# A conv, two gated expert layers on one core: the sums of the weights' maxima leave their PSUM bank by a ScalarE copy

## The chip, the core and the metric

The kernel runs on one core of a Trainium2 chip. The metric is the device time of one execution, in microseconds (us). A core has five engines that run their own queues of instructions in order: TensorE (PE in the profile, with its weight loads as PEld), VectorE (DVE), ScalarE (ACT), GpSimd (POOL) and SyncE (SP, which issues most of the DMAs). They wait for each other by semaphores. TensorE writes its results into PSUM, which has eight banks per partition; all of them are taken here.

## What is computed

```python
out  = causal_conv(x, softmax(weight))         # 8 heads of 24 columns, 7 taps, x is 4 x 3584 x 192
x    = out.reshape(14336, 192)
# layer 1: every row goes to its best of 8 experts
e    = argmax(x @ w_gate)
x    = softmax(x @ w_gate)[e] * (relu(x @ w1[e]) @ w2[e])          # 192 -> 1024 -> 192
# layer 2: the same, and a sigmoid of a second gate
e    = argmax(x @ w_gate2)
out  = softmax(x @ w_gate2)[e] * sigmoid(x @ w_output_gate)[e] * (relu(x @ w1b[e]) @ w2b[e])
```

## The kernel before

Floats are carried as pairs of float16 (a high and a low part), so that a product is three matmuls of 16 bit. For this the weights of all 16 experts (two layers of eight) are split on the core into two halves each, scaled by a power of two that is found from their largest absolute value. One such half (w1 or w2 of an expert) is a unit of `preps`: it is loaded (L273 to L276), ACT takes absolute maxima along the rows (L298, two pieces, tile `wam`), `scale` finds the power of two, ACT and POOL (in the conv also DVE) write the two halves (L325 to L338), SP stores them.

`scale` calls `total` (L140 to L146): two matmuls with a matrix of ones (L145) add the row maxima of the 128 partitions, so that every partition has the sum. The sum, one number a partition, stands in a PSUM tile `total` with tag `lg` of the pool `rps`. `pow2` then makes the scale on the vector engine: a maximum with a tiny number (L131), which reads the sum, then two bit operations (L136, L137). In the conv there are 16 such units (layer 1), in layer 1's expert slots another 16 (layer 2). `gate_weights` calls `total` twice more (`gaam` at the start, `gbam` in the conv; there the first reader is L133).

The tag `lg` has one buffer, one PSUM bank. In turn it holds:
- `total`, freed by its reader L131;
- in the conv, `lg`: the logits of 4 tiles (matmuls L517), freed by DVE's L532;
- in layer 1's slots, `tp`: six transposes of an earlier slot's result (L1186), freed by ACT's copy `ext` (L1192), and `lg`: that result's logits for layer 2 (L1200), freed by DVE's L1211.

A matmul that writes the bank waits until the tile that it held before has been read.

There are three stages. The **conv** (to about 231 us of the trace) runs 32 turns; in turn k TensorE does the conv of tile group k+1 (L465, tile `cxp`, two buffers), then `total` where a unit is at that point, transposes of group k-3 (L507) and logits of group k-4 (L517). DVE scales group k out of `cxp` (L479 to L487, tile `cxs`); L487 frees the buffer that group k+2 wants. ACT makes `chl` from `cxs` (L493, group k-1) and copies transposes out (L510, `cxt`).

The **slots of layer 1** (63, from about 250 us) and of **layer 2** (63 more) are 256 rows of one expert each, or 128 rows. In slot u TensorE runs stage 1 (L1134, 40 matmuls into four banks `ph`), `total` if a unit is due (every third slot), the transposes `tp` of slot u-3, stage 2 of slot u-1 (L1150, 48 matmuls into `py`, two buffers) and the logits `lg` of slot u-4. ACT and DVE empty each `ph` bank (L1136, then L1137), and ACT and DVE bring the result of slot u-1 to the next layer's form (L1160 to L1168). DVE's routing work, which decides what rows later slots take (L613 to L1021), is woven in between: a little after each stage 1, before the unit's L131. The order of all queues is fixed when the program is written (`manual_schedule`): no engine passes over a waiting instruction.

Of the kernel before, what the change touches and what calls it, by code (L numbers as in the profile page):

```python
# [11 lines left out]
F32 = mybir.dt.float32  # L12
# [5 lines left out]
P = 128  # L18
# [37 lines left out]
class Kern:  # L56
# [83 lines left out]
    def total(self, ams):  # L140

        n = ams[0].shape[-1]
        r = self.rps.tile([P, n], F32, tag="lg", name="total")
        for i, am in enumerate(ams):
            self.nc.tensor.matmul(r, lhsT=self.ones32, rhs=am, start=i == 0, stop=i == len(ams) - 1)  # L145
        return r  # L146

    def setup(self):
        nc = self.nc
# [1298 lines left out]
```

## Time and profile before

| | us |
|---|---|
| three runs: median (lowest to highest) | 1367.17 (1366.86 to 1368.79) |
| the profiled execution | 1367.8 |
| its span, first to last instruction | 1366.1 |
| TensorE busy in the span | 1216.8 (89%) |
| VectorE busy | 827.8 (61%) |
| ScalarE busy | 638.2 (47%) |
| GpSimd busy | 614.4 (45%) |

Busy time is what an engine's instructions took; time in which an engine sits before an instruction is named with the instruction that ended the wait (the releaser). "PE tp L1186 <- DVE wst L131" reads: TensorE stood before the matmul that writes `tp`, and L131's end let it go. An engine that is not the bottleneck may sit idle at no cost, so a wait counts only where its engine is the one that the end hangs on.

### The profile page before, as it was taken

What the parts mean: (1) busy time and instruction counts of PE and PEld (TensorE: products, weight loads), DVE (VectorE), ACT (ScalarE), POOL (GpSimd) and SP (SyncE); (2) the same over time, 40 slices, a digit from 0 to 9 for tenths busy, and PEclk for the clock granted to TensorE, in tenths of its full rate; (3) what the DMA queues carried; (4) which work ended last, traced back from release to release, by engine and by line L of the source; (5) the groups of instructions that cost most, each with busy time, mean ns of one, the idle gap of its engine ahead of it and who ended that gap; (6) DMA issues with size and microseconds to landing.
All of it is one profiled execution on the core that took longest, in us unless ns stands there. A gap on an engine that the chain in (4) does not pass through costs nothing. (4 is left out here: it accounts for less than half of the span.)

```text
span 1366.1 us, 36343 instructions
## 1 busy us (share of the span) xinstructions
PE 1216.8 (89%) x13048; PEld 1151.6 (84%) x13048; DVE 827.8 (61%) x2497; ACT 638.2 (47%) x1155; POOL 614.4 (45%) x673
## 2 busy tenths in 40 slices
PE   5867885788998998998787999999999998999997
PEld 4867885687998898997777999999999997899987
DVE  4677689577777655555477775578665444444433
ACT  2756674254655565654554444433333333333332
POOL 5434442324555454453544434344444446344442
PEclk9556555799999999999998999999999999999999
DMA  6989775455556746695684698664344666655374
GB/s 191 276 218 258 200 213 161 117 127 144 138 138 174 185 111 152 163 256 136 179 212 123 163 223 201 155 139 109 92 118 111 152 148 161 159 138 153 93 195 150
DMA packets 251600, 223.12 MB, mean 163 GB/s; under 512 B 144558, under 2 KB 221031, under 8 KB 251416
## 3 DMA queue, kind: packets, MB, share of 16 engines
q1 hardware_dynamic: 231068, 184.32, 51.2%
q0 software_dynamic: 17136, 34.68, 11.8%
q8 instruction: 107, 1.75, 0.6%
q10 hardware_dynamic: 3212, 1.74, 0.5%
q14 instruction: 77, 0.63, 0.2%
HBM read 275.60 MB, written 60.37 MB: 246 GB/s over the span
## 5 line engine op out<-in xcount | busy, mean ns | idle before, releaser
L1134 PE MATMUL ph<-mxt,wb 128*128 128x256 f16 (+1 forms) x4840 | 536.9, 271 | 21.6 <-DMA mxt<-row 10.1
L1134 PEld LDWEIGHTS <-wb 128*128 128x128 f16 x4840 | 457.4, 99 | 74.9 <-issue 12.1
L1150 PE MATMUL py<-wb,h 128*128 128x192 f16 x5592 | 492.4, 249 | 0.0
L1137 DVE SCALAR_TENSOR_TENSOR h<-ph,h 128x512 f16<-128x512 f32 x476 | 314.2, 687 | 286.7 <-ACT h L1136 281.3
L1150 PEld LDWEIGHTS <-h 128*128 128x128 f16 x5592 | 471.9, 99 | 3.4 <-issue 0.3
L1136 ACT ACTIVATE h<-ph 128x512 f16<-128x512 f32 x476 | 274.3, 595 | 176.4 <-PE ph L1134 171.5
L1050 POOL DMA_INDIRECT row<-rec,idx x238 | 233.1, 979 | 87.6 <-issue 44.1
L1233 POOL DMA_INDIRECT out_dram<-o,io x119 | 121.1, 1017 | 232.4 <-ACT o L1232 193.2
L1169 POOL TENSOR_TENSOR ehl<-exs,ehl 128x256 f16<-128x256 f32 (+1 forms) x63 | 42.1, 667 | 296.9 <-ACT ehl L1168 230.5
L1164 ACT ACTIVATE exs<-py,ess 128x192 f32<-128x192 f32 x119 | 44.0, 418 | 204.6 <-DVE ese L137 195.4
L1232 ACT ACTIVATE o<-py,sc 128x192 f32<-128x192 f32 x119 | 44.0, 417 | 199.7 <-PE py L1150 153.0
L465 PE MATMUL cxp<-x,tz 118*112 118x96 f32 x512 | 90.2, 359 | 43.0 <-DVE cxs L487 34.1
L465 PEld LDWEIGHTS cxp<-x,tz 118*112 118x112 f32 x512 | 83.8, 265 | 45.6 <-DVE cxs L487 36.3
L1160 DVE TENSOR_REDUCE eam<-py 128x2 f32<-128x384 f32 (+1 forms) x63 | 33.6, 533 | 124.0 <-PE py L1150 123.9
L338 POOL TENSOR_TENSOR wh<-wr,wh 128x768 f16<-128x768 f32 x48 | 81.2, 1691 | 54.1 <-ACT wh L326 52.8
L1186 PE MATMUL tp<-ident,ehl 128*128 128x128 f16 x357 | 31.8, 226 | 44.6 <-DVE wst L131 43.3
L510 ACT COPY cxt<-ctp 128x1344 f16<-128x1344 f16 x32 | 40.9, 1277 | 60.8 <-PE ctp L507 60.5
L1192 ACT COPY ext<-tp 128x768 f16<-128x768 f16 (+1 forms) x63 | 47.4, 752 | 45.4 <-PE tp L1186 43.6
L1186 PEld LDWEIGHTS <-ehl 128*128 128x128 f16 x357 | 26.9, 104 | 46.9 <-issue 46.1
L494 POOL TENSOR_TENSOR chl<-cxs,chl 112x512 f16<-112x512 f32 x32 | 37.8, 1183 | 41.7 <-ACT chl L493 37.3
L298 ACT ACTIVATE none<-wr 128x768 f16<-128x768 f32 x64 | 53.7, 839 | 1.0
L517 PE MATMUL lg<-gawt,cxt 128*112 128x16 f16 x384 | 35.0, 226 | 5.8 <-DVE L L532 4.7
(203 smaller groups left out, 1087.1 us busy)
## 6 DMA issues: line engine op xcount, KB each, us to landing
wb<-wd SPq DMA_DIRECT2D x126, 768.0 KB
wb<-wda SPq DMA_DIRECT2D x126, 512.0 KB
wb<-wdb SPq DMA_DIRECT2D x126, 256.0 KB
wb<-wdb SPq DMA_DIRECT2D x126, 128.0 KB
wr<-in_moe_w_dram SPq DMA_DIRECT2D x16, 768.0 KB
wd<-wh SPq DMA_DIRECT2D x16, 768.0 KB
rec<-chl SPq DMA_DIRECT2D x32, 336.0 KB
rec<-ehl SPq DMA_DIRECT2D x56, 192.0 KB
```

The source lines that it names most:

```text
L298: nc.scalar.activation(none, u.r[:, c * CH : (c + 1) * CH], AF.Abs, scale=scale, accum_out=u.am[:, c : c + 1])
L338: nc.gpsimd.tensor_tensor(u.h[:, 1, q], u.r[:, q], u.h[:, 0, q], ALU.subtract)
L465: nc.tensor.matmul(to[:, :, hh * GD : (hh + 1) * GD], lhsT=self.tz[: self.KI, h, :], rhs=xin[b0][: self.KI, o : o + G, h * GD : (h + 1) * GD],
L1050: nc.gpsimd.indirect_dma_start(out=rw[:, :], out_offset=None, in_=rec[:, :], in_offset=bass.IndirectOffsetOnAxis(ap=idx, axis=0))
L1134: nc.tensor.matmul(ph[:, k, :], lhsT=l, rhs=xt[:, xb, 0:n], start=i == 0, stop=i == 4)
L1136: nc.scalar.activation(hi, ph, AF.Relu)
L1137: nc.vector.scalar_tensor_tensor(lo, in0=ph, scalar=0.0, in1=hi, op0=ALU.max, op1=ALU.subtract)
L1150: nc.tensor.matmul(py[:, c, 0:D], lhsT=h[:, f, a, c * P : (c + 1) * P], rhs=w[:, b, f, :], start=n == 0, stop=n == 3 * NCH - 1)
L1164: nc.scalar.activation(xs[:, c], py[:, c], AF.Copy, scale=sc[:, c : c + 1])
L1186: nc.tensor.transpose(tp[:, 3 * c + b], hl[:, c, b * P : (b + 1) * P], self.ident)
L1192: nc.scalar.copy(xt, self.sl[u].pop("tp"))
L1233: nc.gpsimd.indirect_dma_start(out=outs[q % NOUT][:, :], out_offset=bass.IndirectOffsetOnAxis(ap=io[:, 0:1], axis=0), in_=o, in_offset=Non ...
```

## The change

`total` no longer returns the PSUM tile. ACT copies it into a small tile `sums` in SBUF (tags `total1` and `total2` by width, four buffers each), and `total` returns that; so L131 and L133 read `sums`. All lines behind are three higher in the changed kernel (L1186 is L1189, L493 is L496).

```diff
@@ def total(self, ams)
             self.nc.tensor.matmul(r, lhsT=self.ones32, rhs=am, start=i == 0, stop=i == len(ams) - 1)
-        return r
+
+        t = self.ew.tile([P, n], F32, tag=f"total{n}", name="sums")
+        self.nc.scalar.copy(t, r)
+        return t
```

ACT has 34 instructions more, one for each call of `total`; on the other engines the order of the arithmetic, the matmuls and the DMAs is as before, and only what they wait for differs. ACT's queue at the first unit in layer 1's slots, before (`exs` and `ehl` are the result of the slot before last, `h` the four `ph` banks, `ext` the copy that frees the transposes):

```order
L1168 CAST ehl<-exs 128x2x192 [waits Activation_49]
L1136 ACTIVATE h<-ph 128x2x256 [waits PE_49] x4
L1192 COPY ext<-tp_3471 128x768 [waits PE_49]
L1164 ACTIVATE exs<-py,ess 128x192 [waits DVE_49,PE_49,Pool_49]
L1164 ACTIVATE exs<-py,ess 128x192
```

and the same place of the changed kernel:

```order
L1171 CAST ehl<-exs 128x2x192 [waits Activation_49]
L1139 ACTIVATE h<-ph 128x2x256 [waits PE_49] x4
L148 COPY sums<-total 128x1 [waits PE_49]
L1195 COPY ext<-tp_3509 128x768 [waits PE_49]
L1167 ACTIVATE exs<-py,ess 128x192 [waits DVE_49,PE_49,Pool_49]
```

The copy stands behind the slot's four `h` and ahead of `ext`. TensorE's queue there, before:

```order
L1134 MATMUL ph<-mxt,wb_0_70 128x256
L145 MATMUL total<-wam,ones_155 128x1 [waits Activation_49]
L145 MATMUL total<-wam,ones_155 128x1
L1186 LDWEIGHTS ehl
L1186 MATMUL tp_3471<-ident,ehl 128x128 [waits DVE_49]
```

and now:

```order
L1137 MATMUL ph<-mxt,wb_0_70 128x256
L145 MATMUL total<-wam,ones_155 128x1 [waits Activation_49]
L145 MATMUL total<-wam,ones_155 128x1
L1189 LDWEIGHTS ehl
L1189 MATMUL tp_3509<-ident,ehl 128x128 [waits Activation_49]
```

No row moved; the first transpose waits for ACT where it waited for DVE. In the conv, ACT's queue around one of layer 1's units (`chl` of group k-1, `cxt` of group k-3), before:

```order
L493 CAST chl<-cxs 112x4x192 [waits DMAHW3_49,DVE_49]
L510 COPY cxt<-ctp 128x1344 [waits PE_49]
L493 CAST chl<-cxs 112x4x192 [waits DMAHW6_49,DVE_49]
L510 COPY cxt<-ctp 128x1344 [waits PE_49]
L325 ACTIVATE wr<-wr,wss 128x768 [waits DVE_49]
```

and now:

```order
L496 CAST chl<-cxs 112x4x192 [waits DMAHW3_49,DVE_49]
L513 COPY cxt<-ctp 128x1344 [waits PE_49]
L148 COPY sums<-total 128x1 [waits PE_49]
L496 CAST chl<-cxs 112x4x192 [waits DMAHW6_49,DVE_49]
L513 COPY cxt<-ctp 128x1344 [waits PE_49]
```

The copy went ahead of the `chl` of its turn. DVE's queue at that unit has the same rows in the same order in both; its L131, which waited for TensorE, now waits for ACT.

## Rows read from the trace of the kernel before

**Rows 1.** Stages: from:to, length, busy us (count) of PE, PEld, DVE, ACT, POOL, granted clock, DMA share, GB/s.
```profile
277.00:745.00 468.00, 416.38 (x4632) 391.96 (x4630) 304.14 (x922) 252.04 (x481) 225.21 (x233) 0.95 0.63 162
745.00:1366.00 621.00, 602.22 (x6699) 568.23 (x6697) 330.65 (x1085) 239.01 (x467) 273.74 (x290) 0.99 0.60 147
```

**Rows 2.** Waits from 277 to 745 us: waiting <- releaser: total us, times, longest.
```profile
PE tp L1186 <- DVE wst L131: 43.3, 16, 6.9
```

**Rows 3.** Timeline, first unit in the slots: start us, duration us, instruction [idle before <- releaser].
```profile
286.18 0.50 PE L145 MATMUL total<-wam,ones 128*128 128x1 f32 x4
286.22 2.47 DVE L1137 SCALAR_TENSOR_TENSOR h<-ph,h 128x512 f16<-128x512 f32 x4
286.38 0.60 ACT L1136 ACTIVATE h<-ph 128x512 f16<-128x512 f32 x1 [0.49 <-PE ph L1134]
...
290.80 0.15 DVE L131 TENSOR_SCALAR wst<-total 128x1 f32<-128x1 f32 x1
291.00 0.59 PE L1186 MATMUL tp<-ident,ehl 128*128 128x128 f16 x6 [4.32 <-DVE wst L131]
...
296.95 0.30 PE L1200 MATMUL lg<-gbwt,ext 128*128 128x32 f16 x6
```

**Rows 4.** Timeline, third unit in the slots.
```profile
352.75 2.25 ACT L1136 ACTIVATE h<-ph 128x512 f16<-128x512 f32 x4
...
354.65 0.58 PE L145 MATMUL total<-wam,ones 128*128 128x1 f32 x4
...
355.97 0.49 PE L1186 MATMUL tp<-ident,ehl 128*128 128x128 f16 x6 [0.74 <-DVE wst L131]
...
360.26 0.30 PE L1200 MATMUL lg<-gbwt,ext 128*128 128x32 f16 x6
```

**Rows 5.** Timeline, last unit in the slots.
```profile
732.31 2.05 ACT L1136 ACTIVATE h<-ph 128x512 f16<-128x512 f32 x4
...
732.44 0.50 PE L145 MATMUL total<-wam,ones 128*128 128x1 f32 x4
...
739.84 0.80 PE L1186 MATMUL tp<-ident,ehl 128*128 128x128 f16 x6 [6.89 <-DVE wst L131]
...
746.72 0.30 PE L1200 MATMUL lg<-gbwt,ext 128*128 128x32 f16 x6
```

**Rows 6.** Timeline, the fifteenth unit: the longest stall after which stage 2 kept its pace.
```profile
706.25 0.33 PE L1186 MATMUL tp<-ident,ehl 128*128 128x128 f16 x3 [3.36 <-DVE wst L131]
...
706.41 4.12 PE L1150 MATMUL py<-wb,h 128*128 128x192 f16 x48
```

**Rows 7.** Stage view of the six us behind the first stall (columns as in rows 1).
```profile
291.00:297.00 6.00, 6.00 (x56) 5.83 (x56) 0.43 (x4) 0.80 (x1) 0.00 (x0) 0.72 0.01 3
```

**Rows 8.** Groups of ACT by line and form: count | busy us, mean ns | idle before <- releaser.
```profile
L1164 ACT ACTIVATE exs<-py,ess 128x192 f32<-128x192 f32 x119 | 44.0, 418 | 204.6 <-DVE ese L137 195.4 <-PE ph L1134 9.2
L768 ACT ACTIVATE zs<-zs 128x16 f32<-128x16 f32 x7 | 1.4, 200 | 0.0
```

**Rows 9.** Waits from 32 to 231 us, the conv (columns as in rows 2).
```profile
DVE wst L131 <- PE total L145: 29.1, 14, 4.0
```

**Rows 10.** Timeline, one conv turn with a unit.
```profile
43.06 0.83 ACT L493 CAST chl<-cxs 112x768 f16<-112x768 f32 x1 [0.38 <-DVE cxs L487]
...
43.08 3.30 PE L465 MATMUL cxp<-x,tz 118*112 118x96 f32 x16 [1.05 <-DVE cxs L487]
...
46.17 0.91 PE L145 MATMUL total<-wam,ones 128*128 128x1 f32 x4
...
47.11 0.16 DVE L131 TENSOR_SCALAR wst<-total 128x1 f32<-128x1 f32 x1 [3.96 <-PE total L145]
...
50.19 0.69 PE L465 MATMUL cxp<-x,tz 118*112 118x96 f32 x2 [0.93 <-DVE cxs L487]
```

**Rows 11.** Timeline, a conv turn in which ACT is busy when the sum ends.
```profile
109.37 0.53 PE L145 MATMUL total<-wam,ones 128*128 128x1 f32 x4
...
110.23 0.19 ACT L298 ACTIVATION_READ_ACCUMULATOR none<-wr 128x1 f32 x1
```

## Prediction, made before the changed kernel was run

> **What bounds the kernel now.** I read the stages first [rows 1]. Layer 2's slots (745 to 1366 us) have TensorE busy for 602.22 of 621 us at a granted clock of 0.99: whatever arrives there earlier ends earlier. Layer 1's slots with units in them (277 to 745 us) have TensorE busy for only 416.38 of 468 us, at 0.95; DVE is busy for 304.14, so over the whole stretch it is no bound. The list of waits says where most of the missing 51.6 us are: 43.3 us, in 16 waits, TensorE stood before the transposes `tp` until DVE's L131 [rows 2]. There are 16 units there, so every one stalls TensorE once.
>
> The first shows how [rows 3]. The sum ends at 286.68 (start and duration of `total`). The transposes want the same bank, and it is free only when L131 has read the sum. L131 stands in DVE's queue behind four L1137 (2.47 us) and routing work, and starts at 290.80; TensorE goes on at 291.00, 4.32 us late. The reader itself takes 0.15 us: the stall is DVE's queue. It is 0.74 us where DVE had nothing else [rows 4] and 6.89 us where routing was long [rows 5].
>
> A long stall costs more than its own time. Behind the first one the granted clock is 0.72 over six us [rows 7], a mixture of the levels 1.2 and 2.4 GHz. From the transposes to the logits L1200 it takes 5.95 us [rows 3], against 4.29 in the undisturbed slot [rows 4]: 1.66 lost; behind the longest it takes 6.88, 2.59 lost [rows 5]. Five stalls, of 4.32 us and more, are of this kind (I took the same difference for each: 1.66, 1.79, 1.97, 2.68, 2.59; 10.7 in all). Behind a stall of 3.36 us stage 2 took 4.12 us at full pace [rows 6]. [...]
>
> **Part one, layer 1's slots: the bank is freed by ACT.** ACT's queue has the copy behind the slot's four `h`, whose last waits for the same stage 1 as the sum does. So TensorE resumes at the later of two times (the sum's end, plus 0.03; the end of ACT's last `h`), plus the copy, plus the hand to TensorE. That hand is 0.05 us (L131 ends at 290.95, the transposes start at 291.00) [rows 3].
>
> The copy, 128x1 out of PSUM, is not in the trace. Its ends: ACT's 128x16 takes 0.20 us and its accumulator read of one column 0.19; ACT's 128x192 out of PSUM takes 0.418 [rows 8, 11]. One column is nearest to the first, I take 0.20, and keep 0.19 and 0.42 for the range. The Trainium skill prices it otherwise: "ScalarE: Activation LUTs", section "Rules for kernel authors", gives about 0.3 us for an ACTIVATE plus a little per element and tells to use VectorE, not ScalarE, for simple arithmetic; by 0.3 us the final sum would be about 3 us worse than by the row. The 0.20 of the 128x16 speaks against that price, and DVE's cheap 0.15 is just what arrives late here.
>
> With 0.20 the 16 new stalls come in three kinds, from the times of each unit as in [rows 3 to 5]:
> - ACT is free when the sum ends, 3 units: 0.03 + 0.20 + 0.05 = 0.28 us (the row: ACT done at 355.00, sum at 355.23 [rows 4]; one of the three is 0.31). Together 0.87.
> - ACT is at its last `h`, 10 units: in the first, ACT ends at 286.98, so TensorE resumes at 287.23, 0.55 us after the sum [rows 3]; the others 0.54 to 0.74. Together 5.9.
> - ACT is late because the slot before kept it, 3 units: in the last, ACT ends at 734.36, TensorE resumes at 734.61, 1.67 us after the sum [rows 5]; the other two 2.2 and 2.3. Together 6.1.
>
> That leaves 12.9 of 43.3 us: **30.4 saved**. No new stall reaches 3.36 us, so the five slow stretches go too: **10.7 saved**.
>
> Does the gain stay? After the transposes TensorE has stage 2 and the logits, 4.29 us [rows 4], before it writes the first `ph` bank again, which DVE's L1137 must have emptied. In the first unit those four end at 288.69 [rows 3], while TensorE would be there at about 291.6; L131 and what is behind it now delay only DVE's own next step, which waits for stage 2 anyway. TensorE's next demand on that bank comes a whole stage 1 later. So I let it all stand. ACT loses nothing: behind the copy stands `ext`, which waits for the transposes in any case.
>
> **Part two, the conv: one more station on a path that already waits.** Here DVE stands before L131 until TensorE's sum ends, 29.1 us in 14 waits [rows 9], and behind L131 in its queue are the scaling steps whose last, L487, TensorE's next conv group waits for. One turn shows the loop closed [rows 10]: L465 starts at 43.08 when L487 lets it, the sum follows, L131 at 47.11, L465 again at 50.19 when the next L487 lets it. The copy comes between sum and L131: 0.20 + 0.05 for 14 units and for the second gate's sum, 15 x 0.25 = 3.75 us. In one turn ACT still is at its absolute maxima when the sum ends (109.90 against 110.42 [rows 11]), another 0.5. In two units DVE came later than the copy will, and nothing is lost. **4.3 us lost**; 0 if the clock or DVE's idle time covers it, 7.6 with a copy of 0.42. At the start `gaam`'s copy stands behind a DMA issue on ACT's queue, but its result is wanted by the first logits only, more than 10 us later: nothing.
>
> The parked copy also holds back `chl`, which stood ahead of it: from 43.06 to about 47.4 [rows 10]. POOL finishes `chl` some 2.7 us after ACT starts it, so at about 50, and the `cxs` buffer that it frees is wanted by the L487 after next, at about 55: covered.
>
> **Sum.** 30.4 + 10.7 - 4.3 = 36.8 us off the profiled execution's 1367.8 (span 1366.1 and 1.7 around it): 1331.0. The median is 0.6 lower, so 1330.4 against it; I say 1331. With a copy of 0.42 us: 16 x 0.22 = 3.5 less in the slots, 3.3 more in the conv, 1337.8. With no loss in the conv: 1326.7.
>
> **The rivals.**
> - *The stall moves on.* DVE is still behind in the long cases, and TensorE meets it at its next wait for DVE, or, running 9% denser, meets its weights' loads. Then the long five give back what they save (19.0 us of the 30.4: 3.8, 2.8, 4.1, 3.1, 5.2) and keep their slow clock: 36.8 - 19.0 - 10.7 = 7.1 saved, 1361; half of that, 1346. For it: DVE's queue was long for up to 6.9 us. Against: the cover of 4.29 us and a whole stage 1 of 4.5 us before the bank is wanted again; the DMA share of 0.63 [rows 1].
> - *Slower: the copy parks ACT in the conv.* ACT waits at the copy for TensorE while `chl`, POOL and the `cxs` buffers wait behind it. If DVE then waits for a buffer in each of the 16 turns, 2.6 us a turn pay back the whole 41.1; at 3 us a turn: +48 - 41 = +7, 1375. For it: `chl` starts 4.3 us later in that turn [rows 10]. Against: the slack of some 5 us worked out above.
> - *The bank isn't freed sooner.* If ACT came as late as DVE, the stalls stay and only the conv pays: 1372. In 13 of the 16 units ACT was done within 0.5 us of the sum, and the queue has nothing between `h` and copy. As the kernel would then be slower, it counts there.
> - *Only a small gain from the conv's jitter* (within 0.2%, some 2.7 us, which is about what a measurement tells from no change): needs a mixture of the above.
>
> **How the numbers follow.** My forecast 0.78, with its own range of 1325 to 1339; the stall moves on, 0.14 (faster in either half); slower by the parked ACT or an unfreed bank, 0.05; no difference, 0.03. So faster 0.92, same 0.03, slower 0.05. The range of 8 in 10 is 1323 to 1347: 3 us under the forecast without a loss in the conv, since the remaining stalls may come out shorter, and up to half of the moved stall.
>
> **What would show it.** In the trace after: the wait of `tp` names ACT's `sums`, 16 times, 13 us instead of 43.3; the copy's mean is near 0.20 us; the granted clock in layer 1's slots rises from 0.95 to about 0.98; in the conv L131 waits for `sums`, some 33 us; the first L1134 comes 4 us later and layer 2's slots have the length that they had. I am wrong if L131's wait is replaced by one for L1137, L1211 or a load in the slots behind, if L487 waits for POOL or ACT in the conv, or if the copy takes 0.4 us.

## The result, and the profile after

| | before | after |
|---|---|---|
| runs: median (lowest to highest), us | 1367.3 (1366.86 to 1368.79), 4 runs | 1326.91 (1326.38 to 1329.2), 4 runs |
| the profiled execution / its span | 1367.8 / 1366.1 | 1326.38 / 1324.6 |
| TensorE busy in the span | 1216.8 (89%) | 1210.8 (91%) |
| first `ph` of layer 1's slots starts | 249.94 | 253.23 |
| last unit's `lg` (L1200, now L1203) starts | 746.72 | 707.39 |

The changed kernel takes 0.9706 of the time of before, interval [0.9689, 0.9723]: 40 us less, where 36 were forecast. First the stages (columns as in rows 1; layer 1's slots now end at 705):

```profile
277.00:705.00 428.00, 409.24 (x4651) 385.47 (x4648) 301.94 (x921) 256.06 (x503) 226.02 (x235) 0.99 0.69 175
705.00:1324.60 619.60, 602.20 (x6709) 568.64 (x6707) 334.24 (x1096) 238.54 (x467) 274.62 (x291) 0.99 0.60 149
```

Against [rows 1] the slots' stage is 40 us shorter at nearly the same busy time of TensorE (409.24 against 416.38), and its granted clock went from 0.95 to 0.99. Layer 2's stage is what it was, to within 1.4 us. TensorE's waits from 277 to 705 us (columns as in rows 2):

```profile
PE tp L1189 <- ACT sums L148: 10.8, 16, 2.1
PE lg L1203 <- ACT ext L1195: 6.1, 3, 3.3
PE ph L1119 <- DVE L L1214: 0.8, 1, 0.8
```

The 43.3 us of [rows 2] are 10.8, again 16 times, now put down to ACT's copy. No new wait above 0.5 us has come in: the wait for `ext` stood in the trace of before with the same 6.1 us, and the one for DVE's `L` with 1.0. The first unit, to be laid beside [rows 3]:

```profile
289.24 0.50 PE L145 MATMUL total<-wam,ones 128*128 128x1 f32 x4
289.28 2.48 DVE L1140 SCALAR_TENSOR_TENSOR h<-ph,h 128x512 f16<-128x512 f32 x4
289.44 0.60 ACT L1139 ACTIVATE h<-ph 128x512 f16<-128x512 f32 x1 [0.49 <-PE ph L1137]
...
289.94 0.15 ACT L148 COPY sums<-total 128x1 f32<-128x1 f32 x1
...
290.14 0.49 PE L1189 MATMUL tp<-ident,ehl 128*128 128x128 f16 x6 [0.39 <-ACT sums L148]
...
290.47 4.12 PE L1153 MATMUL py<-wb,h 128*128 128x192 f16 x48
...
293.86 0.15 DVE L131 TENSOR_SCALAR wst<-sums 128x1 f32<-128x1 f32 x1
...
294.43 0.31 PE L1203 MATMUL lg<-gbwt,ext 128*128 128x32 f16 x6
```

TensorE stands 0.39 us in place of 4.32. DVE reads the sum no earlier than before: L131 starts 4.6 us after the sum begins (289.24 to 293.86), as it did. But stage 2 runs meanwhile, at full pace: 4.29 us from the transposes to the logits, 5.95 before. The last unit, beside [rows 5]:

```profile
700.95 2.05 ACT L1139 ACTIVATE h<-ph 128x512 f16<-128x512 f32 x4
...
701.08 0.50 PE L145 MATMUL total<-wam,ones 128*128 128x1 f32 x4
...
702.87 0.18 ACT L148 COPY sums<-total 128x1 f32<-128x1 f32 x1
703.10 0.50 PE L1189 MATMUL tp<-ident,ehl 128*128 128x128 f16 x6 [1.52 <-ACT sums L148]
...
703.43 4.12 PE L1153 MATMUL py<-wb,h 128*128 128x192 f16 x48
```

1.52 in place of 6.89; here ACT, late from the slot before, sets what is left. The copy itself, as a group (columns as in rows 8):

```profile
L148 ACT COPY sums<-total 128x1 f32<-128x1 f32 x33 | 5.3, 162 | 59.7 <-PE total L145 52.6 <-DMA td<-wv 7.1
```

It takes 0.16 us. In the conv, the waits of 32 to 231 us that answer to [rows 9], and the turn that answers to [rows 10]:

```profile
DVE wst L131 <- ACT sums L148: 35.2, 14, 4.2
DVE wh L337 <- ACT wh L331: 6.8, 5, 1.9
```
```profile
44.50 0.53 PE L145 MATMUL total<-wam,ones 128*128 128x1 f32 x4
...
45.07 0.16 ACT L148 COPY sums<-total 128x1 f32<-128x1 f32 x1 [2.37 <-PE total L145]
45.13 0.83 ACT L496 CAST chl<-cxs 112x768 f16<-112x768 f32 x1
45.26 0.15 DVE L131 TENSOR_SCALAR wst<-sums 128x1 f32<-128x1 f32 x1 [2.33 <-ACT sums L148]
```

The sum ends at 45.03, L131 starts 0.23 us later. It was 0.03 in [rows 10]: the station costs 0.20 us in this turn. L131's waits are 35.2 us, where 29.1 stood in [rows 9]. DVE's list has no wait for POOL or for the `chl` that was held back.

### The profile page after: what moved, and what is told of

Its sections match the earlier page's. It is cut to its first block, busy times and chain, and to the rows that moved or that the text cites. A ratio compares the mean times of both kernels' runs of the same rounds, so it can differ in the third digit from the quotient of the medians.

```text
span 1324.6 us, 36375 instructions
## 1 busy us (share of the span) xinstructions
PE 1210.8 (91%) x13048; PEld 1147.2 (87%) x13048; DVE 825.5 (62%) x2497; ACT 641.6 (48%) x1189; POOL 616.3 (47%) x673
## 4 chain that ended last, share of the span: by engine, by line
PE 73%; DVE 14%; ACT 4%; DMA 3%; issue 3%; SPq 1%; POOL 1%; POOLq 0%; DVEq 0%; ACTq 0%
PE ph L1137 33%; PE py L1153 30%; PE cxp L468 4%; DMA wb<-wdb 2%; DVE h L1140 2%; PE tp L1189 1%; DVE cxs L490 1%; ACT h L1139 1%; DVE cxp L482 1%; DVE wh L337 1%; PE acc L971 1%; PE total L145 1%; DVE eam L1163 1%; DMA rec<-chl 1%; PE ctp L510 1%
## 5 line engine op out<-in xcount | busy, mean ns | idle before, releaser
L1137 PE MATMUL ph<-mxt,wb 128*128 128x256 f16 (+1 forms) x4840 | 536.5, 271 | 20.2 <-DMA mxt<-row 10.1
L1137 PEld LDWEIGHTS <-wb 128*128 128x128 f16 x4840 | 457.1, 99 | 73.4 <-issue 11.5
L1153 PE MATMUL py<-wb,h 128*128 128x192 f16 x5592 | 483.5, 247 | 0.0
L1153 PEld LDWEIGHTS <-h 128*128 128x128 f16 x5592 | 464.0, 98 | 2.1
L1189 PE MATMUL tp<-ident,ehl 128*128 128x128 f16 x357 | 30.4, 220 | 11.9 <-ACT sums L148 10.8
L520 PEld LDWEIGHTS <-cxt 128*112 128x112 f16 x384 | 35.9, 194 | 5.7 <-issue 5.2
```

The source lines that it names most:

```text
L520: nc.tensor.matmul(lg[:CT, g, :], lhsT=xt[:, g * 3 + b, :], rhs=self.ga[0][:, 1 if b == 1 else 0].rearrange("p a e -> p (a e)"), start=b == 0,
L1137: nc.tensor.matmul(ph[:, k, :], lhsT=l, rhs=xt[:, xb, 0:n], start=i == 0, stop=i == 4)
L1153: nc.tensor.matmul(py[:, c, 0:D], lhsT=h[:, f, a, c * P : (c + 1) * P], rhs=w[:, b, f, :], start=n == 0, stop=n == 3 * NCH - 1)
```

## The experiments

They ran on three chips, on which the kernel before took 1370.4 (e1 to e4), 1402.1 (e5 to e7) and 1367.7 us (e8 to e11); so ratios to the kernel before on the same chip are compared. Executions of one kernel on one chip spread over some 3 to 12 us, so the traces carry more of the argument than the times. The table has from each trace the start of the first `ph` of the slots, the start of the last unit's `lg`, the difference of the two, TensorE's wait at `tp` for the unit's sum, and its waits for weight loads (`wb`) between the two. The wait at `tp` is what the profile puts down to the sum's reader; in e5 and e7 it puts a part of the stall down to other ends, and with it the 16 stalls are 13.6 and 19.1 us.

| kernel | ratio, interval | first `ph` | last unit's `lg` | between | wait at `tp` | loads |
|---|---|---|---|---|---|---|
| before | 1 | 249.94 | 746.72 | 496.8 | 43.3 | 0 |
| after | 0.9706 [0.9689, 0.9723] | 253.23 | 707.39 | 454.2 | 10.8 | 0 |
| e1 copy by DVE | 1.0017 [1.0, 1.0035] | 256.47 | 754.36 | 497.9 | 43.3 | 0 |
| e2 in the slots only | 0.9675 [0.9644, 0.9705] | 250.42 | 706.82 | 456.4 | 10.2 | 1.2 |
| e3 in the conv only | 1.0006 [0.9986, 1.0026] | 254.01 | 750.71 | 496.7 | 43.4 | 0 |
| e4 units first | 0.9886 [0.9847, 0.9925] | 251.26 | 736.77 | 485.5 | 30.7 | 0 |
| e5 two copies | 0.970 [0.967, 0.9731] | 253.46 | 716.42 | 463.0 | 9.6 | 1.2 |
| e6 mid copy | 0.9599 [0.9569, 0.9629] | 250.58 | 701.46 | 450.9 | 2.1 | 1.4 |
| e7 mid, DVE reads | 0.9744 [0.9713, 0.9774] | 253.34 | 726.03 | 472.7 | 15.3 | 0.2 |
| e8 after again | 0.969 [0.9669, 0.9712] | 257.18 | 711.46 | 454.3 | 10.8 | 0 |
| e9 slots only again | 0.9704 [0.9684, 0.9723] | 249.83 | 705.25 | 455.4 | 9.7 | 1.6 |
| e10 two copies again | 0.9715 [0.9695, 0.9736] | 253.78 | 708.64 | 454.9 | 11.8 | 0 |
| e11 mid copy again | 0.9657 [0.963, 0.9685] | 251.71 | 701.77 | 450.1 | 1.4 | 2.4 |

**Is it the copy, or whose queue it stands in?** e1 leaves everything as in the changed kernel, but DVE makes the copy.

```diff
-        self.nc.scalar.copy(t, r)
+        self.nc.vector.tensor_copy(t, r)
```

> The changed kernel with the one copy moved from ACT to the vector engine: the sum still goes to a tile of its own and L131 still reads the copy, but the copy stands where L131 stood, at the end of the vector engine's queue. Theory (the gain comes from ACT's shorter queue): TensorE is let go when the vector engine gets there, so the 16 waits before the transposes stay at 43 us, give or take 3, and the conv pays about 0.2 us for each of 15 sums: 1368 to 1372 us. Rival (a copy out of the bank as such gives the gain, whichever engine makes it): waits near 11 us and about 1327 to 1330.

Measured 1372.23 us, ratio 1.0017. TensorE's wait in e1:

```profile
PE tp L1189 <- DVE sums L148: 43.3, 16, 6.9
```

The same 43.3 us, 16 times, longest 6.9 as in [rows 2], though the sum leaves the bank by a copy here too. The copy as such gives nothing; that it stands in ACT's queue, which comes to it sooner than DVE's, gives the gain.

e4 goes the other way: no copy, DVE reads the bank as before, but the unit's step stands ahead of the routing work in its queue.

```diff
+                preps.tick(point)
+                preps.run()
                 work.tick("B")
                 left = work.run(WORK[2])
                 work.tick("A")
-                preps.tick(point)
-                preps.run()
```

> The kernel before, without any copy, but with the vector engine's routing work behind the unit's L131 in each slot and not ahead of it. Theory (the stall is what stands ahead of L131 in that queue): the part of it that is routing goes, the four L1137 and what the slot before left stay. From the times of before that leaves about 32 of 43 us of waits, and some three of the five slow stretches go: 1348 to 1354. Rival (the reader or the bank itself is slow, whatever the queue): 1367.

Measured 1355.75 us, ratio 0.9886. The wait at `tp` is 30.7 us, near the 32 that were expected:

```profile
PE tp L1186 <- DVE wst L131: 30.7, 16, 4.6
```

So the routing work that stood between the four L1137 and L131 explains 12.6 us of the 43.3. What stays is the four L1137, and routing work of the slot before that makes DVE late for them: in the last unit the first L1137 starts at 728.35, 1.97 us after the sum's end. The expectation missed in one point: the slow stretches did not go. From transposes to logits it takes more than 5.7 us in seven of the 16 units. One of them, the fourteenth, is slow in every trace here; of the other six the shortest stall is 1.62 us long:

```profile
470.29 0.50 PE L1186 MATMUL tp<-ident,ehl 128*128 128x128 f16 x6 [1.62 <-DVE wst L131]
470.62 5.78 PE L1150 MATMUL py<-wb,h 128*128 128x192 f16 x48
```

The granted clock over this stretch (470.29 to 476.23 us) is 0.71. So between the marks e4 is only 11.3 us shorter than before, though its waits at `tp` are 12.6 us shorter.

**Which part gives, which costs?** e2 returns the bank itself in the conv and copies in the slots; e3 does the reverse, with `if self.attended`, which is true in the slots of layer 1.

```diff
+        if not self.attended:
+            return r
         t = self.ew.tile([P, n], F32, tag=f"total{n}", name="sums")
```

> The changed kernel with the copy made in the slots of layer 1 only; in the conv, L131 and L133 read the bank themselves as before. Theory (the copy costs the conv 3.3 us, since L131 there stands on the path): the first matmul of the slots starts at about 250 us of the trace where it started at 253.2, the rest is as with the change, 1323 to 1324. Rival (the later start was chance, or is given back later): 1327, the time of the changed kernel.

> The other half of the change: the copy in the conv and at the start only, in the slots L131 reads the bank as before. Theory: only the conv's cost, 1370 to 1371 us, 3.3 above the kernel before; the 16 waits in the slots are 43 us as before. Rival (the two halves help each other, or the conv's cost is chance): 1367.

Measured 1326.21 us for e2 and 1371.12 for e3, ratios 0.9675 and 1.0006. In the table the slots' part has the whole gain (496.8 to some 456), and in e3 all stalls are back. The conv's part moves the first `ph`: from 250.42 to 254.01 between the two. In e3's time it is not resolved: 3.3 us would be a ratio of 1.0024, and the interval [0.9986, 1.0026] holds that as well as 1. Without it e2 should have been 3 us faster than the changed kernel. The ratios, 0.9675 and 0.9706, have overlapping intervals, and the trace of e2 doesn't bear it out: its last unit's `lg` comes at 706.82, 0.6 us before that of after. Two things took the start back. One is a stretch at the lower clock; the second unit of after, then of e2:

```profile
319.34 0.18 ACT L148 COPY sums<-total 128x1 f32<-128x1 f32 x1
319.57 0.50 PE L1189 MATMUL tp<-ident,ehl 128*128 128x128 f16 x6 [2.10 <-ACT sums L148]
319.90 4.12 PE L1153 MATMUL py<-wb,h 128*128 128x192 f16 x48
```
```profile
317.63 0.80 PE L1191 MATMUL tp<-ident,ehl 128*128 128x128 f16 x6 [2.10 <-ACT sums L150]
318.22 5.17 PE L1155 MATMUL py<-wb,h 128*128 128x192 f16 x48
```

The same stall of 2.10 us, and then 48 matmuls in 4.12 and in 5.17 us; the stages behind the stall (320 to 326 us in after, 318 to 324 in e2) were granted

```profile
320.00:326.00 6.00, 6.00 (x75) 5.80 (x72) 4.73 (x17) 1.62 (x4) 2.97 (x2) 1.00 0.65 124
```
```profile
318.00:324.00 6.00, 6.00 (x65) 5.84 (x63) 3.79 (x11) 0.80 (x1) 3.03 (x2) 0.80 0.39 104
```

1.00 and 0.80. The other thing is the loads: TensorE waits 1.2 us for weights in e2, not at all in after.

e9 and e8 are e2 and the changed kernel once more, on one chip.

> The changed kernel, unaltered, beside its three variants on one chip. Two chips have given ratios to the kernel before of 0.9706 (this kernel) and, for its variants, 0.968, 0.970 and 0.960. Expected again 0.970 +-0.002. It is the base for the three that follow.

> The copy only where the sum is taken in layer 1's slots, none in the conv. Theory A (the conv's copy costs 3 us that stay on the path to the end, since the first ph came at 250.4 instead of 253.2): 3 us faster than the kernel with both copies, a difference of 0.2% of the kernel before, so 0.968 if that one is 0.970. Theory B (the slots behind take the gain back, as in the one trace, where the last unit's sum came at 701.15 against 701.08): the same time within 1 us. By B the granted clock falls behind a stall of about 2.1 us at 317 us as in the earlier trace; by A that fall was a matter of that one execution and TensorE runs the next 48 matmuls in 4.1 us.

Measured 1325.28 us for e8 and 1326.5 for e9: without the conv's copy no gain is seen. But five runs of e8 spread over 9 us, so this pair leaves a difference of 3 us open. In e9 the same stall is followed by full pace:

```profile
316.55 0.49 PE L1191 MATMUL tp<-ident,ehl 128*128 128x128 f16 x6 [2.10 <-ACT sums L150]
316.88 4.12 PE L1155 MATMUL py<-wb,h 128*128 128x192 f16 x48
```

So e2's drop does not belong to the kernel; whether it belongs to that execution or to its chip no run tells, since e9 ran on another one. The loads came again: from the first `ph` to the last unit, TensorE's waits in e9 have

```profile
PE ph L1139 <- DMA wb<-wdb: 1.6, 2, 0.8
```

and e8 has no such row. e9 starts the slots 3.4 us before after does and is 2.1 ahead at the last unit; the rest of its lead is not seen in the times, which spread by more than that. e8 shows the spread: the very kernel of after has its first `ph` at 257.18, 4 us later, and needs the same 454.3 us from there. The conv of after, then of e8 (32 to 231 us, columns as in rows 1):

```profile
32.00:231.00 199.00, 152.72 (x1219) 150.09 (x1219) 144.88 (x362) 130.63 (x193) 85.21 (x83) 0.57 0.79 218
```
```profile
32.00:231.00 199.00, 155.90 (x1188) 153.37 (x1187) 141.31 (x348) 129.04 (x191) 85.15 (x83) 0.53 0.78 212
```

The granted clock was 0.57 and 0.53, and e8 got 31 of some 1219 matmuls less done in the same time. Both lie between the two levels, 1.2 GHz (0.5) and 2.4 GHz (1.0), and over all the traces the conv's clock goes from 0.53 to 0.59.

**What does a copy cost?** e5 and e10 put a second copy, into a tile that nobody reads, ahead of the one that is used.

```diff
+        t0 = self.ew.tile([P, n], F32, tag=f"spare{n}", name="spare")
+        self.nc.scalar.copy(t0, r)
         t = self.ew.tile([P, n], F32, tag=f"total{n}", name="sums")
```

> The changed kernel with a second copy of the same kind on ACT ahead of the one that is used (its result is thrown away). Theory (the copy stands on the path in both stages): each of 16 stalls in the slots and of about 15 sums in the conv grows by one copy, 0.16 us, so about 5 us: 1331 to 1333. Rival (ACT's copy is covered in one of the stages or both): 1327 to 1329.

> Each sum is copied twice by ACT, the second result used by nobody behind the first copy's order but before it in the queue: 0.16 us more between sum and release, in 16 slots and 15 times in the conv. Theory 'each copy stands on the path': +31 x 0.16 = 5 us over the kernel with one copy, 0.37% of the kernel before. Rival 'the copy is hidden by what follows': within 1 us. The first ph tells the conv's part: +2.4 us by the theory, 0 by the rival.

Measured 1359.43 us for e5 (0.970) and 1327.34 for e10 (0.9715, beside 0.969 of the changed kernel on that chip): 2 us more with overlapping intervals, where 5 were expected. The trace of e10 says why, at the first unit:

```profile
290.60 0.15 ACT L148 COPY spare<-total 128x1 f32<-128x1 f32 x1
...
290.64 0.18 ACT L150 COPY sums<-total 128x1 f32<-128x1 f32 x1
...
290.87 0.50 PE L1191 MATMUL tp<-ident,ehl 128*128 128x128 f16 x6 [0.46 <-ACT sums L150]
```

The second starts 0.04 us after the first and ends 0.07 after it: the two overlap for 0.11 us. 16 x 0.07 is 1.1, and the wait at `tp` went from 10.8 to 11.8. In the conv nothing can be told: e10's first `ph`, 253.78, lies between the two traces with one copy (253.23 and 257.18). In the slots the copy does stand on the path, but a second one is no second 0.16 us, and this experiment can't price the first.

**Can the rest go too?** e6 and e11 drop the conv's copy, and place the unit's two matmuls ahead of the fourth `ph` bank of stage 1, so that ACT copies behind its third `h`. e7 has the same place without any copy, and DVE reads the bank as before.

```diff
+        if not self.attended:
+            return r
...
-            if u.scaled:
+            if u.scaled and not hasattr(u, "s"):
                 scale(u)
+        def ahead():
+            for u in units:
+                if u.stage == LA + 1 and not hasattr(u, "s"):
+                    scale(u)
+        self.ahead = ahead
...
-            units = [u for u in units if u.stage < len(stages)]
+            units[:] = [u for u in units if u.stage < len(stages)]
...
                 nc.vector.scalar_tensor_tensor(lo, in0=ph, scalar=0.0, in1=hi, op0=ALU.max, op1=ALU.subtract)
+                if f2 == 4:
+                    self.ahead()
```

> The copy by ACT in the slots only, and the sum's matmuls put ahead of the fourth bank of stage 1 (they stood behind it). Theory (what is left of the waits, 11 us, is the copy's place behind the four h of ACT): TensorE has the fourth bank, 1.1 us, to do while ACT copies, so the waits before the transposes fall to 0 to 4 us; with the conv's 3.3 us also back, 1312 to 1318. Rival (TensorE then waits for the bank at the sum, since the logits before have not been read): a wait of about 1 us in each of 16 units at the sum, 1323 or more.

> The same place for the sum, but no copy: the vector engine reads the bank, its L131 ahead of the slot's last L1137 and of the routing work. Theory (the vector engine comes late because of L1137 and the routing work of the slot before, more than because of where the sum stands): waits of some 15 to 30 us stay, two to four of the five slow stretches stay: 1335 to 1352. Rival (only the place of the sum matters, whoever reads it): as with the copy there, 1312 to 1318.

> In the slots the sum's two matmuls stand ahead of the fourth ph bank of stage 1 and ACT's copy behind the third h; no copy in the conv. Theory (what is left of the transposes' stall, 10.8 us, is ACT's last h and its lateness, and the conv's 3 us come back): about 13 us below the changed kernel, ratio 0.960 if that is 0.970. Rival (the earlier gain was the chip's): the same as the changed kernel within 3 us.

Measured 1344.46 us for e6, 1367.31 for e7 (ratios 0.9599 and 0.9744, one chip) and 1319.7 for e11 (0.9657, beside 0.969). The first unit of e11:

```profile
286.64 0.50 PE L145 MATMUL total<-wam,ones 128*128 128x1 f32 x4
287.01 1.25 PE L1146 MATMUL ph<-mxt,wb 128*128 128x256 f16 x10
288.10 0.50 PE L1200 MATMUL tp<-ident,ehl 128*128 128x128 f16 x6
```
```profile
287.34 0.15 ACT L150 COPY sums<-total 128x1 f32<-128x1 f32 x1
```

Here the copy ends during the last bank's ten matmuls and the transposes follow without a stall. e7 tells place from queue once more: at the same place DVE's read still leaves stalls of 19.1 us, 15.3 of them put down to L131, and 22 us more between the two marks than e6. Its ratio, 0.9744, would be 1332 us against 1367.3, 3 us below the range that was expected. e11 is the fastest of these kernels on its chip, by 5.6 us in the medians against e8. That is less than the 13 expected. TensorE's waits from 251 to 702 us say where a part of the rest is; two longer ones, 10.0 us for the first slots' rows and 6.1 for `ext`, are left out here because the other kernels have them too:

```profile
PE total L145 <- DVE L L1225: 1.9, 2, 1.5
PE ph L1146 <- DMA wb<-wdb: 1.7, 3, 0.8
PE tp L1200 <- ACT sums L150: 1.4, 3, 0.9
PE py L1164 <- DMA wb<-wd: 0.8, 1, 0.8
```

The wait at `tp` lost 9.4 us; the weights' loads now take 2.4 that after doesn't have, and the sum, which comes earlier, waits 1.9 at the same bank for DVE's L1225, the reader of the last `lg`; and behind that wait, in the second unit, transposes to logits took 5.52 us and not 4.29. That is 9.4 less 2.4, 1.9 and 1.2, so 3.9; the stretch between the marks is 4.2 us shorter than in e8. On the chip of e5 and e6 the gain over two copies was 15 us, 12.1 of it between the marks; the profiled e5 took 5.94 us instead of 4.29 behind two of its stalls, which e10 did not, so the size there is not settled.

## Why the prediction was right, step by step

Against the profiled executions the span fell by 41.5 us; 36.8 were forecast. By terms:

| term | predicted | measured in after | in e8 |
|---|---|---|---|
| stalls at `tp` | -30.4 (43.3 to 12.9) | -32.5 (to 10.8) | -32.5 |
| slow stretches behind them, and the rest up to the last unit | -10.7 | -10.1 | -10.0 |
| conv, up to the first `ph` | +4.3 | +3.3 | +7.2 |
| behind the last unit's `lg` | 0 | -2.2 | -1.5 |
| sum | -36.8 | -41.5 | -36.8 |

(The second term is the difference between the marks less the first. That e8 hits the sum is chance: its conv was granted a lower clock, and the profiled execution was the slowest of its five.)

- **The mechanism** was right: the reader's place in its queue set the stall. e1 shows it: the same copy in DVE's queue leaves all of it.
- **The stalls** were over-sized by 2.1 us. ACT's copy takes 0.16 us, not the 0.20 of the nearest row, 16 x 0.04 = 0.6. The rest lies in the units with ACT at its last `h`, at first put at 0.54 to 0.74 and measured at 0.39 to 0.59 (4.4 together, not 5.9), and in those where ACT is late, 2.10, 2.03 and 1.52 instead of 2.2, 2.3 and 1.67. In the first unit ACT's last `h` begins at 289.44 and lasts to 290.04, while the copy shows from 289.94: the two overlap by 0.1 us, as the two copies of e10 do. I added whole durations in a row, and in these rows they are not in a row.
- **The Trainium skill's price** ("ScalarE: Activation LUTs", "Rules for kernel authors": about 0.3 us for an ACTIVATE) is given there for one whose bias is a pointer operand. The copy has no such operand, so I set against my row a price that isn't the copy's. The copy took 0.162 us in the mean of 33, and a second one behind it added 0.07. The row of the same section that sends work to VectorE names `relu`, `max`, `min`, `add` and `mul`, not a copy; taken for a copy it would have given e1, which gained nothing.
- **The slow stretches** went, as forecast: from transposes to logits it takes 4.29 us in 13 of the 16 units, 4.12 in one and 2.31 in a unit with a smaller slot. The exception, the fourteenth, took 6.83 us at 643.79, with a stall of only 0.25 and a granted clock of 0.61. It took 6.07 before, at 0.69, behind a stall of 1.00, and I had overlooked it there; in both traces TensorE had waited 2.59 us for `ext` shortly ahead of it. My reason, that no new stall reaches 3.36 us, does not carry the term: in e4 a stall of 1.62 us was followed by 0.71, and one of 2.10 by 0.80 in e2 and by 1.00 in after. The length of a stall alone does not decide it. So this term holds some luck: three stalls of 1.5 to 2.1 us are left in after, and one slow stretch behind such a stall cost e2 1.3 us (5.60 against 4.29).
- **The conv's loss** was over-sized too: 0.20 us in the turn shown and not 0.25 (0.20 x 15 = 3.0), and 3.3 in the one trace. Over all traces the first `ph` starts at 254.3 in the mean with ACT's copy in the conv (253.2 to 257.2, five traces) and at 251.0 without a copy (249.8 to 253.3, seven): 3.3 again, though the two sets overlap and mix chips. What it costs at the end is not resolved, since neither e3 nor e9 beside e8 shows it in the times.
- **Of the rivals** the first had a grain: a denser slot does meet its loads, 1.2 to 2.4 us in the kernels that came earlier still (e2, e6, e9, e11), and none in the changed kernel. The parked ACT did not happen: no wait of DVE for `cxs` in the conv exceeds 0.5 us. The bank was freed sooner.
- **Layer 2's slots** have the length they had within 2.2 us; 1.5 of it are loads that TensorE waited for (11.0 us before, 9.5 after, behind the last unit's `lg`). Why the loads fitted better I did not test.

## What to carry to other kernels

Where one PSUM bank goes from tile to tile, the writer's stall is the place of the reader in its engine's queue and hardly the reader's own time: look for the engine that has nothing ahead of the read when the bank is full, even if it has to make a copy for the one that needs the data. Then see what else can go between writer and next writer, as in e11: moving the write ahead of ten matmuls of other work hid most of the rest of the stall. Part of such a gain can be taken back as the stage gets denser, here by up to 2.4 us of waits for loads. Judge a few us by the stretch between two marks of a trace, since whole times spread by more.

## What was not expected of the hardware

- ACT's small copies overlap: the first is 0.15 us long, and the next starts 0.04 us after it (e10), and a copy shows 0.1 us before the end of the `h` ahead of it (after).
- The same stall of 2.10 us left TensorE at a clock of 1.00 in three executions (after, e8, e9) and was followed by 0.80 in one (e2). In e5 two stalls, of 2.01 and 2.09, were followed by 5.94 us from transposes to logits each, where 4.29 is the full pace. After and e8 passed 2.03 us at 4.29 too. Before passed 3.36 us at full pace, and e4 did not pass 1.62. What decides it, no run here shows.
- Chips differ: the same kernel before took 1367.7 and 1402.1 us. On the slower one TensorE stood before stage 2's matmuls for nothing that the profile shows, 15.3 us in 30 waits of e5, all in layer 2's slots:

```profile
PE py L1155 <- issue: 15.3, 30, 1.1
```

In e10, the same kernel on the faster chip, no such wait is listed. The granted clock from 750 to 1000 us was 1.00 in both, so the clock is not the reason; what it is, no run here shows.
